# An order pass with measured durations, turns in a PSUM tile and a new table of key shifts

## The chip, the cores and the metric

The kernel runs on one core of a Trainium2 chip. A core has five engines with queues of their own: TensorE (PE in the profile; PEld is its weight load), VectorE (DVE), ScalarE (ACT), GpSimd (POOL) and SyncE (SP), which here issues the DMAs. The metric is the time of one execution on the device in microseconds (us).

## The reference

The computation has three parts in a row. The matrices are held in fp32, the weights of the expert layers in 64-bit floats.

```
# attention: q, k, v are 2 x 8 x 1152 x 64; pairs of query rows are averaged (576 rows remain)
q_pool = q.reshape(B, H, S // 2, 2, D).mean(axis=3)
attn   = softmax(q_pool @ k.T / sqrt(D));   x = attn @ v          -> 1152 tokens x 512
# first expert layer: w_in 512 x 2048, w_out 2048 x 512
h = x @ w_in
P = a0 + a1*h + a2*h^2 + a3*h^3;   Q = 1 + |b0|*|h| + |b1|*h^2
x = (P / (Q + 1e-6)) @ w_out
# second expert layer: w_gate and w_val 512 x 1536, w_out 1536 x 512
xn = x / sqrt(mean(x*x) + 1e-6) * rms_g
out = (silu(xn @ w_gate) * (xn @ w_val)) @ w_out
```

## The kernel before

All instructions are written through a scheduling pass in the kernel's own Python. Each piece of work is an `Op` with an engine, a cost in nanoseconds, a key, a function that emits the instructions, the operations it depends on, and the buffers it uses. Some operations have several ways, that is several engines with a cost each. The pass (`order`, from line 398) keeps a clock per engine: it works out when each ready operation could begin (`begin`: the ends of what it depends on plus a hand-over time between the two engines, and the time at which its buffers come free), and emits, engine by engine, the ready operation with the smallest key among those that could begin about as early as the first. What is emitted is a fixed order for every engine; on the chip each engine takes its queue in that order and waits on semaphores. So costs, hand-overs and keys change no instruction, but the order of each queue, and for operations with several ways the engine.

Two long strings steer the pass. `SHIFTS` has a sign per operation, in the order of their creation, which moves the operation's key by a multiple of 250; `WAYS` has a point where the pass may choose the way, or a digit that pins it. 226 of 2624 entries are digits.

`Buf.serial` marks a buffer whose users on different engines take turns in the pass: its last user's end and a hand-over delay the next (in `begin`). Before the change, the tiles `prep`, `av` and `accp` are so marked, and the PSUM tile `hid` of a hidden layer is not.

The stages, in order of time:

- Attention, in 72 tiles of 128 query rows by 1152 keys, two heads to a pair and nine tiles to a pair of heads. Per tile: scores on PE (line 851, into `hid`), the row maximum on DVE (`nm`, line 880), the exponential on ACT (`p`, line 886), transposes on PE (line 902), copies to SBUF (`pt`) on ACT (line 934) or DVE (line 937), and the product with V on PE (`av`, line 1006). PE's order of these is written out: `attention()` chains all of a pair's score, transpose and V operations by dependences. Not in that chain are the transposes of keys and queries (`prep`, line 800) and of the reciprocal sums. Two `hid` tiles alternate.
- Beside the attention the expert weights are loaded and split from 64-bit floats into a high and a low part (lines 175 to 236; `W_STEPS`, `S_STEPS`): those of the first layer beyond the first few are written back to DRAM ("spill") and fetched later.
- First expert layer (`rational`): 16 hidden units of 128 columns by 1152 tokens. PE makes the hidden tile (`hid`, three matmuls per product since high and low parts are multiplied); ACT and DVE read it in turn (lines 1195 and 1198 on ACT; 1201, 1204 and 1211 on DVE), then work on in SBUF (1214 to 1235), and ACT and POOL (or DVE) make the high and low part of the result (1243, 1246). PE multiplies these by `w_out` into `accp`, and DVE adds that to `acc` (line 1301). For the first two units (`FINE`) and two others the work goes by thirds of 384 columns, each in a PSUM bank of its own, declared independent by bank.
- Norm (`norm`, lines 1356 to 1405): squares, a sum on PE, a root on ACT and four small POOL operations (`o_nr`), broadcast by PE.
- Second expert layer (`gated`, `out2`): 12 units of the same size.

PE works on fp32r operands; a 384-column matmul of the expert layers takes about 0.17 us from start to start.

Of the kernel before, what the change touches and what calls it, by code (L numbers as in the profile page):

```python
# [19 lines left out]
def attention_moe_moe2_kernel(  # L20
# [18 lines left out]
    nc = tc.nc  # L39
    B, H, S, D = q.shape  # L40
# [8 lines left out]
    NU2 = DFF2 // 128  # L49
# [207 lines left out]
    S_STEPS += [("ACT", 625, s_hi), ("POOL", 1230, s_lo), ("SP", 1460, s_store)]  # L257
# [3 lines left out]
    if wide:  # L261
        W_STEPS += [("ACT", 680, w_abs), ("DVE", Port(345), w_shift), ("DVE", Port(620), w_sign), ("DVE", Port(620), w_rest)]
# [13 lines left out]
    def weight(w, u):  # L276
# [13 lines left out]
        "]ZAOQF(:O/TPHZGUPNQOPjLPR=?P@PKSPcPPXSPKEPPI]8PYLPZPPC]WB<POPTPDRPPYLUCFHLm=JPJLV`*JP1PPXMPP<PPWFKPP"  # L290
        "alKWPEcj[DO]PIHPNTFJPZFMHM/,aSPP8GVPWJLQ]KKLRHPYITdcPLhcCiPPZMPXXbP:<LL[>[_PT_PPRCPPPNaPH=MCPPRL;PZK"
        "P[T]QKRK@KOQ@CS_U@O/QXMQ_J9PQS`PIMPX^>6APdYFPLPvPMKCFVRON:ZE]CiLNCcPPyD>PO[XCLXfkPG^PP^WZSFP_E0T2kSN"
        "IMb(PPMMPPYPPPd4J:HP(PXPy8VQMTPSEMIE8RPQQbG>`UANARWOcNPP]LSPN]NNQJt;JwPMOPV]hCPUNUVQF__YPlPOthUPYS<]"
        "PH]YYP[U`(VT;QNNUsY]NA_FXZAPPWJSXTRVQCPbPPZWGFhTPVMbkhTJVP>eY>PJLPPPPOTY2PE]PPFSOVFDJNNQ>PCYPa;iPBPS"
        "[PfPL^TATPXP=LWP_B<OY>P=PVI6WaPXKPcPTPYPhZPOPPaSHPHPJPOPEERRfJX`2TdOaOVPHM^5TUOUPbPPdQPJK[>ORH6P@PBJ"
        "QQKOQDPYPHNZCSFRPOKEWPEPUGPPMPCaP_bPPPbQKFZEWaPKPCZUPRPPVEMV7R[`QRPPR_GOQHQ5PDeU`C?BLNW^O+T^PIPHNRSK"
        "PPMIPPPGPY`PfvLPPRRRPUJU:GLXV^MZLPY^IycPESiP=TJ^PPaTRQ/PZ>-EKIPmcPE;NKOEvuPJFnNQH`TCTUeUBMYPSH;?6OSZ"
        "PVSW[PP9W>_IOgUJ^mOQ3GNDTPKIPhFP[RPBVIJP[6^<XJwPPPSYEVBI.PWARQPQULDDJZJWTSf1NW=FPPKkeFWPJPQP8aPFPOBF"
        "PX@V>RIETfGPKPWPSLPI(^JqIIPaPYSPlNP^PAPn)]G`ZPRNEWPU<]y9PPRNyRAFPDA;EV^W^P?NIW]PMJ^UTPTIKKLUPbUS_MO["
        "NYc]WPRNIIPPPKIQUJPVFDTCKIPPuHM<TPHbT[VKF[QhMWPPPKPWLtYE_aPaNaoR_JVlMPPfrQPPPPWL>RPKUPKEPQLI(PV:H^RJ"  # L300
        ";SENX(GP7Pd9]F^TU[MP5MHQbP_PTV7PZ:XJP(=UNPP_PdPYP?[POHBTUFLOM[KNWVXK;SwNU;L2TP[C[PPj>XUJPPMPJ]@LF`ZM"
        "KWv]P_^QdGb.aWE[[JIPTKJVQ2ITEOAP0]PIRL_O7LZE@^QBLPPXON`:TMKgOQPRFPPNPjKbPTSNSEPP@P<uTPJXWOQPOb`VPe@P"
        "FUQfPUPXPPTPKUGF>jLCI^MEZ=JPSOP?IZVPeP(GMRPSMLnVJPPUPPK;PJKOB9`VGP(Q[LZPLKZEPRMTHWPPNPQCGPPHFY9LYPBP"
        "^GO@fPW[UQirIRULJPPPMPRSPSQPH^SZHPG=TQ(OXYOV=ADPWPWLhVTKYQKHRUP?XZ^cPNN5PQZR.DYP6]^XLQNVAWY;CUP`QPPL"
        "QNOKPNbEOPPPFaPWEIfPPZMPPUI=OPZCPQ<d;IPQWCPRMOQe`NH>PRQHPBPOQH`WNP@PVMP`JPfJTNPR_Pe<PJPJMPXPCVPPOP:P"
        "KOJPVcIOnhPyPQPPXKPILPUPZ=PfPMhMJP9bPPDJPSPJFPfQZ=ZTWPRKPKOHPRTNS@PQKPLUJQSPT3RYoPVVUPP>PIQDMPVnNXPD"
        "PPR`OOPVPBOT]^VAGFMLOiHPPJcLIMPQKRYPYFd`P?WUOPMPY?PQPKUXXS_Z[RdP@PNQUIm`ePPRX_XPxPLHPPXPAPLSPJO;ohYy"
        "POSO`P[E7PP2LMZ(PNaMPMyVRn]CLRRXJ=MGPFSJEP3pPPPE@PXZPPpPSQSaPhfYUPJPaLRX[PSEZIU>USIYUP(PA<KPJPfPIPPI"
        "OPWPxPPPL3GC^URLUQOIPMQLPIU8J5tXPbIWPP=qGUJTUCPPPDLV^VPUT_BVPNK@PPPIOPM9H[DP^PPOPMfPGXPN_J]?@APPKVQE"
# [398 lines left out]
    def head_ops(i):  # L708
# [30 lines left out]
        def f_add(eng):  # L739
# [6 lines left out]
            [(POOL, 1500, lambda: f_add(nc.gpsimd)), (DVE, Port(cost(DVE, m)), lambda: f_add(nc.vector))],  # L746
# [84 lines left out]
    def tile_ops(i):  # L831
# [62 lines left out]

        NB = NKT - 1
# [700 lines left out]
```

## Time and profile before

| | us |
|---|---|
| median of 3 runs (lowest to highest) | 708.67 (706.51 to 709.95) |
| the profiled execution | 706.74 |
| its span, first to last instruction | 705.0 |
| PE busy | 683.8 (97%) |
| PEld busy | 595.3 (84%) |
| DVE busy | 544.1 (77%) |
| ACT busy | 397.0 (56%) |
| POOL busy | 246.6 (35%) |

The shares are of the span. Busy time of PE is the time in which at least one matmul was in flight by its record; the records' ends are modelled, so a short wait may lie inside busy time. A wait is the idle time of an engine before an instruction, put down to whatever came last of what that instruction waited for. The attention takes the first 258 us, the first expert layer goes to about 434, the norm to 482, and the second expert layer to the end.

### The profile page before, as it was taken

The numbers are of one execution on the slowest core, as the hardware profiler recorded it, in microseconds if no ns is written. First come the engines' busy times: TensorE is split into PE (matmuls) and PEld (weight loads), VectorE is DVE, ScalarE is ACT, GpSimd is POOL, SyncE is SP. The second block draws the span as 40 slices with busy tenths as digits, with TensorE's granted clock in tenths as the row PEclk, the third lists the DMA queues.
The fourth block names the chain that finished last, engine by engine and source line by source line (L and its number), as shares of the span: only waits on it lengthen the run. The fifth ranks groups of instructions, "written<-read, shape, count | busy, mean of one in ns | idle before, by whom it ended". The sixth has DMA issues, their size and how long they took to land.

```text
span 705.0 us, 13072 instructions
## 1 busy us (share of the span) xinstructions
PE 683.8 (97%) x5257; PEld 595.3 (84%) x5257; DVE 544.1 (77%) x724; ACT 397.0 (56%) x624; POOL 246.6 (35%) x246
## 2 busy tenths in 40 slices
PE   8899999999999999999999999999999999999997
PEld 7576767667776778999999999999999899989996
DVE  5789998898888876999968989867778155983944
ACT  3676787888788876978646566346333232311310
POOL 1124346666546674311111253344222012422500
PEclk9999999999999999999999999999999999999999
DMA  7443436656555436115105005000325012340103
GB/s 209 127 130 101 142 100 193 197 177 228 176 189 181 157 125 215 60 61 164 44 24 186 31 6 174 31 1 1 119 91 160 20 60 89 91 150 0 60 1 134
DMA packets 53900, 77.66 MB, mean 110 GB/s; under 512 B 6480, under 2 KB 36176, under 8 KB 53840
## 3 DMA queue, kind: packets, MB, share of 16 engines
q1 hardware_dynamic: 53840, 76.83, 33.7%
q8 instruction: 41, 0.67, 0.4%
q14 instruction: 19, 0.16, 0.1%
HBM read 62.40 MB, written 14.42 MB: 109 GB/s over the span
## 4 chain that ended last, share of the span: by engine, by line
PE 76%; DVE 14%; ACT 7%; issue 2%; POOL 1%; DVEq 0%; ACTq 0%; POOLq 0%
PE hid L590 24%; PE accp L590 19%; PE hid L851 11%; PE av L1006 10%; PE hid L902 7%; PE prep L800 3%; DVE m_q L1211 2%; ACT p L886 2%; DVE m_p L1201 2%; DVE m_p L1204 2%; DVE m_q L1226 2%; DVE nm L880 1%; DVE m_p L1232 1%; ACT m_u L1195 1%; DVE m_p L1235 1%
## 5 line engine op out<-in xcount | busy, mean ns | idle before, releaser
L590 PE MATMUL hid<-x_hi,win_hi 128*128 128x384 f32 x480 | 161.2, 336 | 4.2 <-issue 2.1
L590 PE MATMUL hid<-x_hi,win_lo 128*128 128x384 f32 x480 | 160.6, 335 | 0.0
L590 PE MATMUL hid<-x_lo,win_hi 128*128 128x384 f32 x480 | 155.4, 335 | 0.0
L880 DVE TENSOR_REDUCE nm<-hid 128x1 f32<-128x1152 f32 x72 | 95.1, 1354 | 15.0 <-PE hid L851 14.6
L886 ACT ACTIVATE p<-hid,nm 128x1152 f32<-128x1152 f32 x72 | 87.9, 1221 | 29.5 <-DVE nm L880 29.3
L590 PEld LDWEIGHTS hid<-x_hi,win_hi 128*128 128x128 f32 x480 | 90.2, 188 | 6.6 <-issue 4.5
L851 PE MATMUL hid<-kT,qT 64*128 64x256 f32 (+3 forms) x800 | 94.0, 380 | 0.1
L590 PEld LDWEIGHTS hid<-x_lo,win_hi 128*128 128x128 f32 x480 | 89.6, 188 | 1.0
L590 PEld LDWEIGHTS hid<-x_hi,win_lo 128*128 128x128 f32 x480 | 90.1, 188 | 0.0
L902 PEld LDWEIGHTS hid<-ident,p 64*128 64x128 f32 x1296 | 52.7, 140 | 34.8 <-issue 13.7
L1246 POOL TENSOR_TENSOR g_lo<-m_p,g_hi 128x1152 fp32r<-128x1152 f32 (+1 forms) x16 | 37.8, 2368 | 125.8 <-ACT g_hi L1243 79.4
L851 PEld LDWEIGHTS hid<-kT,qT 64*128 64x128 f32 (+1 forms) x800 | 70.2, 182 | 9.1 <-issue 1.7
L1006 PE MATMUL av<-pt,vn 128*64 128x288 f32 x576 | 76.7, 411 | 0.0
L902 PE MATMUL hid<-ident,p 64*128 64x64 f32 x1296 | 66.2, 230 | 9.0 <-ACT p L886 8.3
L934 ACT ACTIVATE pt<-hid 128x512 f32<-128x512 f32 (+2 forms) x129 | 57.4, 473 | 24.7 <-PE hid L902 23.0
L175 ACT ACTIVATE wc<-wraw 128x512 f32<-128x512 f32 x68 | 45.8, 673 | 39.2 <-POOL win_lo L208 18.1
L590 PE MATMUL accp<-g_hi,wout_hi 128*128 128x384 f32 x192 | 65.3, 340 | 1.2 <-DVE acc L1301 1.2
L937 DVE COPY pt<-hid 128x512 f32<-128x512 f32 (+2 forms) x95 | 50.5, 548 | 18.7 <-PE hid L902 17.0
L590 PE MATMUL accp<-g_lo,wout_hi 128*128 128x384 f32 x192 | 64.3, 335 | 0.4 <-POOL g_lo L1246 0.4
L590 PE MATMUL accp<-g_hi,wout_lo 128*128 128x384 f32 x192 | 64.2, 335 | 0.0
L1006 PEld LDWEIGHTS av<-pt,vn 128*64 128x64 f32 x576 | 38.6, 136 | 27.0 <-issue 3.3
L1455 ACT ACTIVATE m_p<-hid 128x1152 f32<-128x1152 f32 (+1 forms) x14 | 14.0, 997 | 57.9 <-PE hid L590 57.8
(120 smaller groups left out, 1231.9 us busy)
## 6 DMA issues: line engine op xcount, KB each, us to landing
wraw<-in_moe_w_out_dram SPq DMA_DIRECT2D x28, 512.0 KB, 3.5
far<-spill SPq DMA_DIRECT2D x23, 512.0 KB, 3.1
wraw<-in_moe_w_in_dram SPq DMA_DIRECT2D x16, 512.0 KB, 3.9
wraw<-in_moe_w_gate_dram SPq DMA_DIRECT2D x12, 512.0 KB, 3.8
wraw<-in_moe_w_val_dram SPq DMA_DIRECT2D x12, 512.0 KB, 3.6
kn<-in_k_dram SPq DMA_DIRECT2D x16, 288.0 KB, 4.0
vn<-in_v_dram SPq DMA_DIRECT2D x16, 288.0 KB, 3.3
qn<-in_q_dram SPq DMA_DIRECT2D x16, 256.0 KB, 3.1
```

Of the source, the lines that this page charges most:

```text
L175: nc.scalar.activation(c.bitcast(F32), wt["raw", n][:, :, 1].bitcast(F32), AF.Abs, scale=2.0**-112)
L590: ins = nc.tensor.matmul(dst, lhsT=a[x], rhs=b[y], start=first and i == 0 and p == 0, stop=last and i == n - 1 and p == len(by) - 1,)
L800: seen(nc.tensor.transpose(ps[:, at:at + 128], src, ident))
L851: ins = nc.tensor.matmul(ps[to, j, c:c + x1 - x0], lhsT=qT[2 * pr + h][rows, c0:c0 + to.stop - to.start], rhs=kT[2 * pr + h][rows, x0:x1], ...
L880: nc.vector.tensor_reduce(out=e["nm"], in_=scores(), op=ALU.max, axis=AX.X, negate=True)
L886: nc.scalar.activation(e["p"], scores(), AF.Exp, bias=e["nm"], scale=1.0, accum_out=sums[pr][:, t:t + 1])
L902: ins = nc.tensor.transpose(ps[:, g, c:c + 64], e["p"][rows, 128 * j:128 * j + 128], ident[rows, rows])
L934: return nc.scalar.activation(to, src, AF.Copy)
L937: return nc.vector.tensor_copy(to, src)
L1006: nc.tensor.matmul(e["av", h][64 * c:64 * c + 64, 0:QW], lhsT=v_tile[2 * pr + h][:, KEYS[kt], :], rhs=pt[pr, h][:, kt, c * QW:(c + 1) * QW ...
L1201: by_bank(nc.vector.tensor_mul(as3(p_(), cs), as3(p_(), cs), h_()))
L1246: eng.tensor_sub(g_(1), p_(), g_(0).bitcast(F32))
```

## The change

The diff touches the pass and its inputs. No function that emits instructions is altered.

- Costs of operations: the weight steps, the query addition (`o_qa`), the row maximum, the exponential, the copies of the transposed tile on ACT and DVE, the spread of the reciprocals (`o_rx`), ACT's absolute value in the first expert layer (`o_aq`), POOL's low part (`o_lo`) and the norm's POOL chain (`o_nr`).
- Hand-over times become a table by pair of engines; a switch of PE between kinds of matmul is booked at 140 instead of 100.
- `project_ops` marks the hidden tile's buffer as serial unless the layer is one that goes by banks (`by_banks`).
- `SHIFTS` and `WAYS` are new throughout; 240 entries of `WAYS` are digits.

```diff
-            ("ACT", 680, w_abs), ("ACT", 680, w_pm), ("DVE", Port(345), w_shift), ("DVE", Port(620), w_rest_kept),
-            ("POOL", 1250, w_times),
+            ("ACT", 630, w_abs), ("ACT", 560, w_pm), ("DVE", Port(410), w_shift), ("DVE", Port(620), w_rest_kept),
+            ("POOL", 1310, w_times),
...
     SHIFTS = (
-        "]ZAOQF(:O/TPHZGUPNQOPjLPR=?P@PKSPcPPXSPKEPPI]8PYLPZPPC]WB<POPTPDRPPYLUCFHLm=JPJLV`*JP1PPXMPP<PPWFKPP"
+        "HPBOSTaTYHCTNONaP4PDPCZIPTuFM2oOLPPPZIUBDNPfPWPKUvXHI7Q<PNPLP@FLIR?UcUPPAPYPPfca]XUXPdAIjNNWPP[LPUPS"
...
-    SWITCH = 100
+    SWITCH = 140
...
+    HANDOFF = {
+        "PE": {"DVE": 220, "ACT": 200, "POOL": 150},
+        "DVE": {"PE": 250, "DVE": 110, "ACT": 92, "POOL": 221},
+        "ACT": {"PE": 265, "DVE": 118, "ACT": 110, "POOL": 190},
+        "POOL": {"PE": 110, "DVE": 55, "ACT": 120, "POOL": 65},
+        "SP": {"PE": 2110, "DVE": 2000, "ACT": 2000, "POOL": 2000},
+    }
+
     def handoff(a, b):
-
-        if a == b:
-            return {DVE: 127, ACT: 143, POOL: 96}.get(a, 0)
-        return 2000 if a == "SP" else {PE: 196, ACT: 160, DVE: 140, POOL: 75, "SP": 100}[a] + (110 if b == PE else 0)
+        return HANDOFF[a].get(b, 0 if a == b else 196 if a == "PE" else 100)
...
         ps = ps or Buf("hid")
+        ps.serial = not by_banks(w, u)
...
+    def by_banks(w, u):
+        return w == "in" and u in FINE or (w, u) in (("gate", 0), ("val", NU2 - 1))
+
     def bank_access(w, u, c, ins):
-        if w == "in" and u in FINE or (w, u) in (("gate", 0), ("val", NU2 - 1)):
+        if by_banks(w, u):
...
-            [(POOL, 1500, lambda: f_add(nc.gpsimd)), (DVE, Port(cost(DVE, m)), lambda: f_add(nc.vector))],
+            [(POOL, 1640, lambda: f_add(nc.gpsimd)), (DVE, Port(cost(DVE, m)), lambda: f_add(nc.vector))],
...
-        o_red = Op(DVE, 1350, key + -2500, f_red, o_qk, [nb])
-        o_exp = Op(ACT, 1430, key + 2400, f_exp, [o_red], [nb, pb, sb])
+        o_red = Op(DVE, 1300, key + -2500, f_red, o_qk, [nb])
+        o_exp = Op(ACT, 1263, key + 2400, f_exp, [o_red], [nb, pb, sb])
...
-                [(ACT, 70 + 1.09 * w + n2, lambda n_=n_: f_out(n_, by_act)), (DVE, 80 + 1.16 * w + n2, lambda n_=n_: f_out(n_, by_dve))],
+                [(ACT, 60 + 0.85 * w + n2, lambda n_=n_: f_out(n_, by_act)), (DVE, 80 + 1.03 * w + n2, lambda n_=n_: f_out(n_, by_dve))],
...
-        o_rx = Op(POOL, 1050, kr + 300, f_rx, [o_rinv], [rb, rxb])
+        o_rx = Op(POOL, 1200, kr + 300, f_rx, [o_rinv], [rb, rxb])
...
-            o_aq = Op(ACT, cost(ACT, n), k + 2000, f_aq, [o_q], [bq])
+            o_aq = Op(ACT, cost(ACT, n) + 110, k + 2000, f_aq, [o_q], [bq])
...
-            o_lo = Op(POOL, cost(POOL, n), k + 5000, f_lo, [o_hi], [bp, *g], [(DVE, Port(cost(DVE, n)), lambda: f_lo(nc.vector))])
+            o_lo = Op(POOL, cost(POOL, n) + 120, k + 5000, f_lo, [o_hi], [bp, *g], [(DVE, Port(cost(DVE, n)), lambda: f_lo(nc.vector))])
...
-        o_nr = Op(POOL, 400, key, f_nr, [o_ms, o_rs], [br])
+        o_nr = Op(POOL, 1050, key, f_nr, [o_ms, o_rs], [br])
```

## Rows read from the trace of the kernel before

**Rows 1.** Busy time (and instructions) of each engine by stage; PEclk is the granted clock.

```profile
0.00:32.00 32.00, 26.30 (x248) 21.47 (x248) 19.89 (x34) 15.02 (x29) 5.71 (x11) 0.89 0.57 161
32.00:258.00 226.00, 220.79 (x2603) 158.02 (x2602) 196.46 (x294) 179.12 (x342) 118.74 (x132) 1.00 0.51 165
258.00:300.00 42.00, 38.82 (x231) 35.83 (x232) 33.25 (x57) 32.47 (x56) 18.92 (x20) 1.00 0.37 126
300.00:434.00 134.00, 131.52 (x748) 128.97 (x747) 117.20 (x107) 87.17 (x81) 32.09 (x12) 1.00 0.26 86
434.00:482.00 48.00, 47.24 (x278) 45.81 (x276) 36.57 (x58) 21.46 (x36) 18.15 (x24) 1.00 0.08 25
482.00:700.00 218.00, 218.00 (x1153) 204.56 (x1154) 139.54 (x177) 61.74 (x83) 52.98 (x49) 1.00 0.24 75
700.00:705.00 5.00, 1.16 (x6) 0.62 (x4) 1.22 (x2) 0.00 (x0) 0.00 (x0) 1.00 0.42 157
```

**Rows 2.** Groups of instructions, 32 to 258 us: busy, mean ns, idle before and releasers.

```profile
L880 DVE TENSOR_REDUCE nm<-hid 128x1 f32<-128x1152 f32 x66 | 87.2, 1354 | 11.9 <-PE hid L851 11.5
L886 ACT ACTIVATE p<-hid,nm 128x1152 f32<-128x1152 f32 x66 | 80.6, 1221 | 24.2 <-DVE nm L880 24.0
L902 PE MATMUL hid<-ident,p 64*128 64x64 f32 x1187 | 59.8, 228 | 4.5 <-ACT p L886 3.7 <-DVE pt L937 0.2
L902 PEld LDWEIGHTS hid<-ident,p 64*128 64x128 f32 x1187 | 47.7, 139 | 28.0 <-issue 12.8 <-ACT p L886 7.4 <-DVE pt L937 3.7
```

**Rows 3.** Instructions in order of time near 87.7 us: start, length, idle before.

```profile
87.68 2.62 DVE L880 TENSOR_REDUCE nm<-hid 128x1 f32<-128x1152 f32 x2 [0.37 <-PE hid L851]
...
89.08 1.22 ACT L886 ACTIVATE p<-hid,nm 128x1152 f32<-128x1152 f32 x1 [1.54 <-DVE nm L880]
...
90.34 1.22 ACT L886 ACTIVATE p<-hid,nm 128x1152 f32<-128x1152 f32 x1
90.44 0.78 PE L902 MATMUL hid<-ident,p 64*128 64x64 f32 x17 [1.01 <-ACT p L886]
```

**Rows 4.** Waits of PE, 258 to 300 us: total, times, longest.

```profile
PE hid L590 <- issue: 1.2, 1, 1.2
PE hid L590 <- DVE m_p L1204: 1.2, 1, 1.2
PE hid L590 <- DVE pt L937: 0.9, 1, 0.9
```

**Rows 5.** Waits, 300 to 434 us.

```profile
DVE m_p L1204 <- ACT m_u L1195: 4.3, 4, 1.3
...
PE hid L590 <- issue: 0.9, 2, 0.5
```

**Rows 6.** Groups by form, 0 to 258 us: the 512-column copies.

```profile
L934 ACT ACTIVATE pt<-hid 128x512 f32<-128x512 f32 x81 | 46.9, 596 | 15.8 <-PE hid L902 15.0
L937 DVE COPY pt<-hid 128x512 f32<-128x512 f32 x62 | 42.2, 689 | 14.4 <-PE hid L902 13.2 <-ACT p L886 0.5
```

**Rows 7.** DVE in order of time at 287.8 us.

```profile
287.78 1.41 DVE L1211 SCALAR_TENSOR_TENSOR m_q<-m_u,absb,hid 128x1152 f32<-128x1152 f32 x1 [0.45 <-ACT m_p L1198]
```

**Rows 8.** Waits of PE, 434 to 482 us.

```profile
PE hid L1389 <- POOL small L1385: 0.6, 2, 0.4
```

**Rows 9.** Busy time in two stretches of the ramp (columns as in rows 1).

```profile
10.00:13.40 3.40, 1.57 (x33) 1.19 (x33) 2.75 (x4) 3.04 (x6) 1.54 (x1) 1.00 0.83 274
13.40:16.90 3.50, 3.50 (x29) 3.17 (x27) 1.38 (x3) 1.07 (x4) 0.00 (x0) 0.51 0.67 180
```

**Rows 10.** DVE and POOL in order of time at 397 us.

```profile
395.90 1.35 DVE L1201 TENSOR_TENSOR m_p<-m_p,hid 128x1152 f32<-128x1152 f32 x1
...
397.17 3.94 POOL L1246 TENSOR_TENSOR g_lo<-m_p,g_hi 128x1152 fp32r<-128x1152 f32 x1 [11.12 <-ACT g_hi L1243]
...
398.96 3.36 DVE L1226 SCALAR_TENSOR_TENSOR m_q<-m_q,m_u 128x1152 f32<-128x1152 f32 x1
```

**Rows 11.** Groups by form, 275 to 450 us.

```profile
L1226 DVE SCALAR_TENSOR_TENSOR m_q<-m_q,m_u 128x1152 f32<-128x1152 f32 x14 | 20.9, 1493 | 0.0
```

More of the change, by code (lines that the diff above doesn't have):

```diff
@@ L253, in attention_moe_moe2_kernel @@
         S_STEPS += [
-            ("ACT", 680, w_abs), ("ACT", 680, w_pm), ("DVE", Port(345), w_shift), ("DVE", Port(620), w_rest_kept),
-            ("POOL", 1250, w_times),
+            ("ACT", 630, w_abs), ("ACT", 560, w_pm), ("DVE", Port(410), w_shift), ("DVE", Port(620), w_rest_kept),
+            ("POOL", 1310, w_times),
         ]
-    S_STEPS += [("ACT", 625, s_hi), ("POOL", 1230, s_lo), ("SP", 1460, s_store)]
+    S_STEPS += [("ACT", 625, s_hi), ("POOL", 1170, s_lo), ("SP", 1460, s_store)]
     W_STEPS = [("SP", 1460, w_load)]
     if wide:
-        W_STEPS += [("ACT", 680, w_abs), ("DVE", Port(345), w_shift), ("DVE", Port(620), w_sign), ("DVE", Port(620), w_rest)]
+        W_STEPS += [("ACT", 560, w_abs), ("DVE", Port(410), w_shift), ("DVE", Port(620), w_sign), ("DVE", Port(620), w_rest)]
     W_STEPS += [("ACT", 620, w_hi), ("POOL", 1230, w_lo)]
@@ L295, in attention_moe_moe2_kernel @@
[L295 to L309, printed above, removed]
@@ new lines, in attention_moe_moe2_kernel @@
+        "OPZNpLDTSsCPROPPPQFIUPWYPPTXPkPx`B=KHpICXPPieO0PLWXMPBJLTGUTPK8RQQVfY+G4QQcQTRQ>P19UGQPPQLP]E^POP2<X"
+        ")RTPJahLL)TTOPSPOPT_POPQLMSeJ>WIBUHKXP]`PG@PKP8n(V3ZAdPGQMPPPP=QTVPVPYPVAaVTAYYPQS>KOB?PMOPaeI_cPG=I"
+        "?OWLPJPLPbPIXKIKGRPWREN]POPdPNXPNP]PXJ]JN`RWPPMSSP[DO[gfPN4_PSQTHPPRPAPPXPPNNPYYPU^HPSPnM[TRP[;bPPdU"
+        "G<YIPUZMMPNJPP8Pi3qYY*;HPPNTPPPwcPFPPJPOJf(M(SOOPO^PYTfNSbMeLfPDlbPPSYBgQ;JMPO8e`:WKPHPPRLTNPQPQUPTH"
+        "NES9JP=MHPIQPBIWEFPAWGQFTXPMPNNM1cPsPPRGCJVMPAMLPySD>Ke4(_P6PkLoNPYsFRPPDMQr`I[TTr^faRVOPDPECJRVPPN0"
@@ new lines, in attention_moe_moe2_kernel @@
+        "PVPTIPD1IYPDKYJR5P@b7_oDXdMYyCDIBWTFp>RNDCwZPO_VNMBOPVPEPPPH^WROScM`PBUHOSImJeYqK4QPMPlNggLKf^F^SWWR"
+        "ENVGcGXJWWL[^XNSPU`VPGPTPCNRPDQRPKNZIiSPCHS]PPdQUIPKZ8SP;SMRYbnYWfLKPd5[VSPUNW;PYE`SXDMId(OXOPPPIOGP"
+        "MVMYPMPiGHMULZ[M=XnOUWJUIOmP^A4UJKSJPPGSV9PGIPUL:PPKPmPQPPPPPRVVYPAQPdd;HMPPHsP<PCKPPPyEHP?FSPNrWR=R"
+        "PPOPTO>P_RPLUPMUP7GRViPDRnPM@DZ_jUC:cYIQPPIT`PPR<OTMNA=7_JDQPe`kNPO>IhXMGPQPIJ@erPWHPP=`PO^bMFPCVXXP"
+        "PGMNPpGKr@PQPRBHPE(L^PJPP9UOPPKKNVPJPPUYZKPP`PWlNPJLUFPV^OqJJ<LBbKAPFDMTLPJ@PPWPRdPSNPPZPL5XPHPUIPQH"
@@ new lines, in attention_moe_moe2_kernel @@
+        "L]`TPP:NPQPHNPXPIPTM=QPLEENPP.PXKYaAtyBPU[S;PVENZTPsPPfLLLZPOHC`l=PLPPKPUDPPAVVSPO?NLPWeSdPPLEQTyKP>"
+        "UQ@JPPPRVPOgKFiLcNPNM_PQPWVOZHFfNPPNORPSbPPKPPhKP^Y[GPO@JOKV0PVTPPPPFUPPOJMKc9@NsM7ePKPmHJ[PeU:OcPXS"
+        "^LC^P[APPPPpYJIJ]TPGWCISHBPRT]P8_cN7XPPLD[URkPUSHPPRPrDW;SOIVUPAWcP:QP6fJD:RLPPPSPKV?PPbnYSRRJ0FMNPP"
+        "OGCJPUBLZUfPXbGL^PSKGQXJPIpPZUTDP@RYLPAdQLabNaLPP[8NPJ@RP7HfPPXKPMPPOPL3APCPEPP+AvVXJ]EQLRPYPXOPVL^J"
+        "HcLPXTXPPMfIPGP.TMPiH^PNPWUJu=PPJNJHP[S`VKhYPPTR<P_ZDP[PBWH_kLHNMPI]Bl9QPBZIHLBPPPMFPPPPoI?NXH7[VPyY"
@@ new lines, in attention_moe_moe2_kernel @@
+        "VREPNPO^VjHGPPFWc`URTaPK(6PIAWRSPE]TYN^ahNSOPN4>KPI[NPFRQfLvXPPPNPGS`PbM6PSOPCaPWGNUQWPPWUYKYH(PLRNP"
+        "PPePRoPPKRSPPPPKPQLH@La3TB;TNARCRbPPPOULY^LKQSbQR^QOSKS`MW@@LiPLPPPSYNRPUWmQKLZPP8MUUH8ZiRLUVRSPT6>h"
+        "p(aWP>PLKZ@TJSLHP3SJPP[`NPQDKSGJPZPMDNPGPOfPGKd[?PRPPXP)@]BNS=JPP@PU^PPLPZIJSP]S`bBhPPIQLPPQKQPVSFPP"
+        "j<PPPVLPUZP]VPR^XOMBaXgSRRvWPZZPDIYbRPIEJPqPR@PET>;iPPOhUQMNPEPTPPTMfFMPPODHALAR<>`JQFL[PPPP(SVPPNQO"
+        "PQ^PCPhCSSYXRSJGQtPdPPUSYZUPUOYP`FQU<cVPcFPSPPBW^LHP[EGWJROOAa?NU]TPMP;LUTPbXAHSPPbPX5Z@=PFXXOT3gZ`C"
@@ new lines, in attention_moe_moe2_kernel @@
+        "0....................1.....1.0......0.10.....1.00.....1..0.......................0.................."
+        "...0........1..0.....0...................1........0......1.01.....1..............01.........0.....01"
+        "0.................1.....0..........0......1.0........0........1......1.0.....................0......"
+        "....00....01......1........1........1..0.......01.................0.......00........1.......00......"
+        ".....1..........0...............1........................0.10.....0.11.................0............"
@@ new lines, in attention_moe_moe2_kernel @@
+        "..0..............00.......................0.1.........1..............0..0........0........1........1"
+        ".......01.....0.1.......................0......0......0.1.........0.....0..0.....1.0........1......0"
+        "..0........1.......00.......1.............1.........0.......1.....0..........0......0........1......"
+        "..0.1......1.0.................1........1.......................11....010........0......11.....20..."
+        "..10.....1......0.......1......0.................................................1........1........."
```

49 lines of the change are left out of this document (17 added, 32 removed).

## The prediction

> **What bounds the kernel now.** Read first the table of busy time by stage [rows 1]. TensorE (PE) is busy 683.83 of 705.00 us. That table also says where it is not, and this is all that another order can win, since no instruction of PE is added or taken away. Before 32 us it is idle 32.00 - 26.30 = 5.70 us; in the rest of the attention 226.00 - 220.79 = 5.21; at the hand-over to the first expert layer 42.00 - 38.82 = 3.18; in the first expert layer 134.00 - 131.52 = 2.48; around the norm 0.76; in the second expert layer (482 to 700 us) 0.00; and in the tail 3.84. Sum 21.17 us, 3% of the span. In the same rows the reader sees who comes next: in the attention DVE with 196.46 of 226 us (87%) and ACT with 179.12 (79%), in the first expert layer DVE with 117.20 of 134 (87%), in the second nobody.
>
> Then the waits. In the attention after the ramp PE's largest wait is that of the transposes for the exponential, 3.7 us; the exponential in turn waited 24.0 us for the row maximum, and the maximum 11.5 us for the scores [rows 2]. The chain scores, maximum, exponential, transpose can be seen once in full at 87.7 us: two maxima in 2.62 us, begun 0.37 us after DVE had run dry, two exponentials 1.26 us apart, and PE 1.01 us idle [rows 3]. At the hand-over PE waits three times about a microsecond before a hidden tile, twice for a reader on DVE and once for nothing that the profile names [rows 4]. In the first expert layer its waits are short, 0.5 us the longest of those for a hidden tile [rows 5].
>
> **The change part by part.** No edit alters an instruction: they alter what the scheduling pass believes and prefers. Instructions move on their engines' queues, the DMA issues on SP's among them, and, where an operation has several ways, between DVE, ACT and POOL. PE's order of scores, transposes and attention-times-V is a chain of dependences that the diff leaves alone, so in the attention only the small transposes of keys, queries and reciprocals can move to fill PE's holes.
>
> *Durations.* The diff books the exponential at 1263 instead of 1430, the maximum at 1300 instead of 1350, the ACT copy of 512 columns at 60 + 0.85 x 512 = 495 instead of 628, DVE's at 607 instead of 674. The rows give the exponential's step from start to start as 90.34 - 89.08 = 1.26 us and the maximum's as 2.62 / 2 = 1.31 [rows 3]. Two maxima of 1354 ns by record [rows 2] thus take 2.62 us and not 2.71: records overlap by about 90 ns, and the copies of 596 and 689 ns [rows 6] occupy about 0.51 and 0.60. The new numbers are close to the trace. The old pass thus booked ACT too high in the attention by 72 x 0.167 + 81 x 0.133 = 22.8 us, and DVE by 72 x 0.05 + 62 x 0.067 = 7.8 us. It saw ACT full where ACT is at 79%, and left DVE, the engine that really is nearly full, with 62 of the large copies. The new one can move copies to ACT and sees true lengths of the chain. What PE can get from it is bounded by its 5.21 us. But DVE was already idle when the maximum of rows 3 became ready (0.37 us), so at such a place only a filler on PE helps, and the old pass with its longer exponential had reason to place one there. I take 2.0 of the 5.21; the ends are 0 and 5.2.
>
> *Turns in a PSUM tile.* At 287.78 us DVE's m_q waits 0.45 us for ACT's m_p (line 1198), whose result it does not use: both read the hidden tile, and one goes after the other [rows 7]. In the first expert layer DVE's line 1204 waited 4.3 us in 4 waits for ACT's line 1195, again another reader of that tile [rows 5]. The old pass did not know of this; the new one plans around it. It cannot free more PE time than PE loses: 3.18 at the hand-over, where 1.2 and 0.9 us of it hang on DVE's reading of the tile [rows 4], and 2.48 after. The two first layers are read by thirds, which the diff leaves without turns, so at the hand-over the gain must come from a better order of DVE's 33.25 busy us. I take half of each: 1.6 and 1.2; the ends are 0 and 3.2, 0 and 2.5.
>
> *Norm and remaining constants.* The norm's POOL chain is booked at 1050 instead of 400; PE's wait for it is 0.6 us [rows 8], of 0.76 idle. I take 0.3. The switch of PE's mode (140 for 100), the cost of the query addition, of the spread reciprocals and of the weight preparation belong to engines with room: POOL is busy 118.74 of 226 us in the attention, and in the second expert layer PE loses nothing. I cost them at 0, with rival 3 below for where their cover ends.
>
> *The ramp.* Before 32 us there is nothing else to do while the first chains run. After a stretch in which PE was busy only 1.57 of 3.40 us, 3.5 us went by at a granted clock of 0.51, that is at 1.2 instead of 2.4 GHz [rows 9]; the 0.89 of the whole ramp [rows 1] is two of these, 2 x 3.5 x 0.49 = 3.4 of 32 us. A new order can win or add one such stretch, 3.5 x 0.49 = 1.7 us either way. I take 0.
>
> *The table made anew.* It holds as many entries as before; 240 instead of 226 pin a way. How good the search was can't be read from anything here; this is why I take about half of what is open and not all.
>
> Sum: 2.0 + 1.6 + 1.2 + 0.3 = 5.1 us, nothing in the second expert layer and in the tail (the last eviction and store remain). The profiled execution took 706.74 us; it becomes 701.6. The median of the runs shown is 708.67, on which the same sum gives 703.6. Not knowing which of the two the next median resembles, I predict the middle, 702.6. Half a per cent, 3.5 us, is about what a measurement here can tell from no change: the three runs alone spread over 3.4 us. The bounds of the parts give from 0 to 5.2 + 3.2 + 2.5 + 0.8 + 1.7 = 13.4 us of gain, and 1.7 of loss.
>
> **The rivals.**
>
> 1. *More is open than PE's idle time shows.* PE's ends are modelled, so short holes hide in busy time. The weight loads show them: in the attention they waited 7.4 us for the exponential and 3.7 for a DVE copy, 11.1 against PE's 3.9 for the same two [rows 2]. If half of the 11.1 and all of 3.18 + 2.48 + 0.76 come back, the gain is 12.0 us, and the time on the middle scale 695.7. Beside this the Trainium skill, "Perfetto Trace Analysis", section "Identifying the Most-Contended Engine", says that TensorE's headroom is to be judged by the busy share of its weight loads and not by that of its matmuls. By that rule the attention with 158.02 of 226 us (70%) has far more room than the second expert layer with 204.56 of 218 (94%). I follow it only so far: an attention load of 0.14 us stands for a matmul of other shape than an expert one, so the share differs without any hole. Against the rival: the chain at 87.7 us shows PE waiting on latency, not on order.
>
> 2. *Nothing to be seen.* What the pass gets right lies beside PE's path: the turns delay DVE by some microseconds, but DVE has 134 - 117.20 = 16.8 us free in that stage, and PE's waits are many short ones that another order only puts elsewhere. For it: PE at 97%. Time: 708.
>
> 3. *Slower: DVE and POOL block each other in the first expert layer.* At 397 us POOL's g_lo and DVE's m_q (line 1226) overlap; m_q takes 3.36 us where a 1152-column step that meets nobody, that at 395.90, took 1.35, so one meeting costs DVE 2.0 us [rows 10]. The group's mean of 1493 ns over 14 shows that such meetings are rare in this order: 14 x (1.493 - 1.35) = 2.0 us in all, one such meeting [rows 11]. The new pass redraws which operations meet, and books POOL longer by 120 without moving it. DVE stands before PE here through the hidden tile's release and the accumulator's additions; the layers' buffers take up one delay, so it decides from about the fourth further meeting in neighbouring layers on. With six meetings more, 12 us on DVE, of which half are taken up, the kernel is 6 us slower: 714. The Trainium skill, "SBUF — State Buffer", section "Who interferes with whom", says that DVE with two SBUF inputs and POOL hold their shared port for a whole instruction and that the order of issue decides who is blocked. By that rule a new order alone can bring this rival; the trace agrees, since m_q has two SBUF inputs. Against it: the pass carries such a term, before and after.
>
> **How the numbers follow.** Forecast (698 to 705) 0.49; rival 1 (below 698) 0.10; rival 2 (705 to 712, by the noise also a small gain or loss) 0.26; rival 3 (above 712) 0.15. Faster by over half a per cent means below 705.1: 0.49 + 0.10 = 0.59, of which I give 0.01 to the border; same 0.27; slower 0.15. For 8 in 10 the range runs from 695.5, which takes in rival 1's own time, to 712, which leaves out rival 3.
>
> **What the profile after would show.** If right: PE idle at 32 to 258 us down to about 3.2, at the hand-over to about 1.6, no wait of PE for a hidden tile over a microsecond there; more than 81 large copies on ACT and fewer than 62 on DVE; DVE's wait of 4.3 us on line 1204 mostly gone; the second expert layer and the tail unchanged. Rival 1 shows as weight loads in the attention waiting less than 7.4 us for the exponential. Rival 3 shows as means of lines 1226 and 1232 well above 1.5 us together with PE waits for DVE. The forecast is wrong if PE's idle time outside ramp and tail (11.6 us) does not fall by three or more, or if the time moves by more than this idle time does.

## The result and the profile after

The kernel after takes 699.29 us (median of 6 runs, 696.55 to 700.77), the kernel before beside it 709.62 (6 runs, 706.51 to 711.56): a ratio of 0.985, 95% interval 0.982 to 0.988. It is faster, and the predicted 702.6 is 3.3 us too high. The time lies inside the predicted range, but that range (695.5 to 712) is wide and held the kernel before as well. On another chip a replay of the same queues took 699.8 against 705.64, a ratio of 0.992 (0.990 to 0.994). The medians of before differ by the clocks that its executions were granted and by a meeting of two engines, told of below. At about one clock (0.995 in the mean over the span for before, 0.994 for after) the second chip's runs of before lie at 706.8 to 707.3 and those of after at 699.1 to 700.0. The profiled executions agree: 706.74 against 699.88, 6.9 us less.

Where the time went is read from three moments in the timeline of PE (start, length, operation, idle before): the first hidden matmul of the first expert layer, and the first and last matmul that projects its result into `accp`. First before, then after.

```profile
258.76 0.41 PE L590 MATMUL hid<-x_hi,win_hi 128*128 128x384 f32 x1 [0.89 <-DVE pt L937]
...
284.55 0.33 PE L590 MATMUL accp<-g_hi,wout_hi 128*128 128x384 f32 x1
...
473.85 0.33 PE L590 MATMUL accp<-g_hi,wout_lo 128*128 128x384 f32 x1
```

```profile
257.57 0.44 PE L596 MATMUL hid<-x_hi,win_hi 128*128 128x384 f32 x1 [0.45 <-ACT pt L943]
...
283.52 0.33 PE L596 MATMUL accp<-g_hi,wout_hi 128*128 128x384 f32 x1
...
467.21 0.34 PE L596 MATMUL accp<-g_hi,wout_lo 128*128 128x384 f32 x1
```

The attention ends 1.2 us earlier. From the first hidden matmul to the first projection it is 25.8 us before and 25.9 after: nothing. From the first projection to the last it is 189.3 and 183.7: 5.6 us, most of the 6.9. Behind it the stages keep their lengths (231.2 and 230.9 us to the end). In the table of busy time by stage, the counterpart of [rows 1], the stages are cut where after has them:

```profile
0.00:32.00 32.00, 25.69 (x243) 21.01 (x245) 19.89 (x36) 14.52 (x28) 2.64 (x9) 0.89 0.60 173
32.00:257.00 225.00, 219.63 (x2609) 158.03 (x2605) 200.13 (x290) 189.42 (x369) 116.51 (x123) 1.00 0.52 167
257.00:300.00 43.00, 40.81 (x245) 37.56 (x242) 33.03 (x55) 31.70 (x56) 10.64 (x12) 1.00 0.36 118
300.00:430.00 130.00, 130.00 (x752) 129.87 (x751) 116.22 (x105) 88.25 (x83) 28.86 (x12) 1.00 0.26 86
430.00:475.00 45.00, 44.38 (x262) 43.36 (x261) 37.08 (x58) 20.73 (x34) 16.19 (x21) 1.00 0.08 24
475.00:693.00 218.00, 218.00 (x1156) 204.59 (x1155) 137.65 (x186) 63.06 (x87) 40.87 (x38) 1.00 0.24 75
693.00:698.10 5.10, 1.28 (x6) 0.74 (x4) 1.34 (x2) 0.00 (x0) 0.00 (x0) 0.86 0.41 154
```

The second number in a row is PE's busy time, the third that of the weight loads. In the first expert layer PE is idle for 0.00 us, where it was for 2.48. That is less than half of the 5.6 us. The rest is in the third number: the loads were idle for 134.00 - 128.97 = 5.03 us before [rows 1], and are for 0.13 after. Most short holes lay under the modelled ends of matmuls, and the loads, which run back to back here, showed them. Between the first and the last projection the loads are busy for 181.84 us before and for 182.26 after, and idle for 7.46 and 1.43: the stretch is as long as the loads' work, which stays, and their holes, which go. In the attention PE is idle for 5.37 us, and was for 5.21. ACT works 10 us more there and DVE 4 us more; PE's idle time hardly moves with it.

The waits of the first expert layer from 300 us on (engine and line, what it waited for, total, times, longest) say who sets the pace. PE has none left; those of [rows 5] were the counterpart. Lines after are 9 higher.

```profile
ACT m_u L1204 <- PE hid L596: 16.6, 6, 8.3
...
ACT m_q L1223 <- DVE m_q L1220: 6.2, 5, 2.6
DVE acc L1310 <- PE accp L596: 5.2, 5, 2.5
DVE m_q L1220 <- ACT m_u L1204: 3.7, 2, 2.8
```

The wait of 4.3 us of DVE's third reading for ACT's absolute value (L1204 for L1195 before) is gone. A smaller one, 3.7 us, stands at the second polynomial's reading (L1220), which needs the absolute value itself. ACT and DVE now wait for PE. At the hand-over (257 to 300 us) the three waits of [rows 4] have become 1.3, 0.4 and 0.4:

```profile
PE hid L596 <- DVE m_p L1213: 1.3, 1, 1.3
PE hid L596 <- ACT pt L943: 0.4, 1, 0.4
PE hid L596 <- issue: 0.4, 1, 0.4
```

In the attention the waits and groups of [rows 2, 6] have these counterparts (32 to 257 us; the copies from 0 to 257): PE still waits for the exponential, 4.0 us, and of the large copies ACT makes 83 for 81 and DVE 59 for 62. Over the whole program, with the small ones, eight went from DVE to ACT (129 to 137 on ACT, 95 to 87 on DVE).

```profile
L911 PE MATMUL hid<-ident,p 64*128 64x64 f32 x1187 | 60.0, 228 | 5.3 <-ACT p L895 4.0 <-DVE pt L946 1.0
```

```profile
L943 ACT ACTIVATE pt<-hid 128x512 f32<-128x512 f32 x83 | 47.6, 596 | 7.1 <-PE hid L911 6.3
L946 DVE COPY pt<-hid 128x512 f32<-128x512 f32 x59 | 39.7, 688 | 13.6 <-PE hid L911 7.2 <-ACT wraw L215 3.6 <-ACT wc L175 1.6
```

### The profile page after: what moved, and what is told of

It is laid out like the page before. It is cut to its first block, busy times and chain, and to the rows that moved or that the text cites. A ratio compares the mean times of both kernels' runs of the same rounds, so it can differ in the third digit from the quotient of the medians.

```text
span 698.1 us, 13067 instructions
## 1 busy us (share of the span) xinstructions
PE 679.8 (97%) x5257; PEld 595.2 (85%) x5257; DVE 545.3 (78%) x728; ACT 407.7 (58%) x652; POOL 215.7 (31%) x214
## 4 chain that ended last, share of the span: by engine, by line
PE 88%; DVE 5%; ACT 4%; issue 1%; DMA 1%; SPq 0%; POOL 0%; DVEq 0%; ACTq 0%; POOLq 0%
PE hid L596 35%; PE accp L596 24%; PE hid L860 10%; PE av L1015 9%; PE hid L911 7%; PE prep L809 3%; ACT p L895 2%; DVE nm L889 2%; DVE pt L946 1%; DMA qn<-in_q_dram 1%; PE prep L1062 0%; ACT pt L943 0%; DVE qp L751 0%; DVE acc L1404 0%; DVE m_p L1210 0%
## 5 line engine op out<-in xcount | busy, mean ns | idle before, releaser
L1255 POOL TENSOR_TENSOR g_lo<-m_p,g_hi 128x1152 fp32r<-128x1152 f32 (+1 forms) x15 | 34.0, 2272 | 124.2 <-ACT g_hi L1252 96.2
L943 ACT ACTIVATE pt<-hid 128x512 f32<-128x512 f32 (+2 forms) x137 | 60.4, 470 | 16.0 <-PE hid L911 14.6
L946 DVE COPY pt<-hid 128x512 f32<-128x512 f32 (+2 forms) x87 | 46.3, 556 | 16.0 <-PE hid L911 9.2
L208 POOL TENSOR_TENSOR win_lo<-wc,win_hi 128x512 fp32r<-128x512 f32 x17 | 23.2, 1367 | 96.8 <-ACT win_hi L201 87.0
```

The lines of the kernel that those rows point to most:

```text
L208: eng.tensor_sub(lo, w_float(n), hi.bitcast(F32))
L943: return nc.scalar.activation(to, src, AF.Copy)
L946: return nc.vector.tensor_copy(to, src)
L1255: eng.tensor_sub(g_(1), p_(), g_(0).bitcast(F32))
```

## The experiments

In most of these kernels the pass does not choose: it replays a list of operations, each with the way that was taken, recorded from the pass of before or of after. So a part of one order can be put into the other, or one operation exchanged with its neighbour. The replay of after unchanged is the last pair below. Line numbers of such kernels are higher; operations and tiles are the same. "Before" stands for the runs of the kernel before on the same chip: 708.77 us (25 runs) for e1_att, e2_rest, t_before and t_after; 708.53 (19) for flat_old, flat_new, c_before and fill_after; 705.64 (18, the second chip) for dve_light, att_light, again_after and fill_again. A ratio compares all runs of a set and is not always that of the two medians.

**The two halves apart.** e1_att takes the attention's queues from after and the rest from before, e2_rest the other way round.

```diff
-            (each step picks the best ready operation by begin() and key)
+            e1_att:  QUEUES = after's entries of the attention, then before's of all the rest
+            e2_rest: QUEUES = before's entries of the attention, then after's of all the rest
```

> Every engine's queue up to the end of the attention as in the changed kernel, every queue after it as in the kernel before (the two orders are written out and replayed, nothing else differs). Theory (the gain lies in the first expert layer): the first hidden matmul of the expert layers starts about 1.2 us earlier as in the changed kernel, and all of the rest keeps the holes of before; 1.2 us faster than before. Rival (an earlier or otherwise ordered attention sets up the expert layer): 4 us or more faster.

> The reverse: queues of the attention as before, queues after it as in the changed kernel. Theory (expert layer): PE without a hole from 300 to 434 us, 5.6 us faster than before, the end of the attention unchanged near 258.8 us. Rival (the two halves only work together): under 3 us faster, with PE holes in the expert layer.

e1_att: 705.94 us (12 runs), ratio 0.998 (0.996 to 1.000), 0.0021 x 708.77 = 1.5 us below before. The interval reaches no change at all, and the 1.2 us of one pair of profiles can't carry it either: one and the same queue of before's attention brought the first hidden matmul at 256.86 to 259.01 us in five profiles (before, t_before, c_before, e2_rest, dve_light), with a clock in the first 32 us of 0.89 to 1.00. Runs at one clock show it better. At 0.995 those of before fall into two groups, 706.4 to 706.9 and 708.6 to 709.0 us, and those of e1_att into 705.7 to 705.8 and 707.4 to 707.8: 0.9 and 1.2 us less. So the attention's share is about 1 us. In its profile the first expert layer still has holes, and one is large. DVE and POOL in order of time, and the matmul that was late:

```profile
395.48 2.66 POOL L1352 TENSOR_TENSOR g_lo<-m_p,g_hi 128x1152 fp32r<-128x1152 f32 x1 [11.11 <-ACT g_hi L1349]
395.48 3.87 DVE L1338 SCALAR_TENSOR_TENSOR m_p<-m_p,ncoef,m_u 128x1152 f32<-128x1152 f32 x1
...
399.28 0.54 DVE L1407 TENSOR_TENSOR acc<-acc,accp 128x384 f32<-128x384 f32 x1
...
399.87 0.44 PE L693 MATMUL accp<-g_hi,wout_hi 128*128 128x384 f32 x1 [2.29 <-DVE acc L1407]
```

This is the meeting of [rows 10], in which the same two operations began within 10 ns of each other. [rows 10] has POOL's, at 397.17 us; DVE's, in the kernel before, is this one:

```profile
397.16 1.41 DVE L1232 SCALAR_TENSOR_TENSOR m_p<-m_p,ncoef,m_u 128x1152 f32<-128x1152 f32 x1
```

There DVE's step came through in 1.41 us and POOL's took 3.94. Here POOL took 2.66 and DVE 3.87: the addition behind DVE's step came late, and PE stood for 2.29 us. Before has this coin toss in its order; its profiled execution had won it.

e2_rest: 706.19 us (12 runs, one of them of 2030 us for no reason that is known), ratio 0.997 (0.995 to 0.999), 2.3 us below before. The total missed the 5.6 us that were expected, the layer did not. From 300 to 434 us its row, and the waits at its seam (257 to 300 us):

```profile
300.00:434.00 134.00, 134.00 (x775) 133.88 (x774) 120.22 (x109) 91.03 (x86) 28.92 (x12) 1.00 0.25 87
```

```profile
PE hid L693 <- DVE m_p L1310: 6.4, 1, 6.4
DVE m_p L1307 <- ACT m_p L1304: 5.1, 1, 5.1
...
ACT wc L175 <- DMA wraw<-in_moe_w_gate_dram: 3.6, 1, 3.6
```

The layer runs without a hole, 183.7 us from first to last projection as in after, so its 5.6 us come from its own order and not from the attention's. But where the two recorded halves meet, a weight step on ACT now stands ahead of the layer's first steps and waits 3.6 us for its DMA. PE stops for 6.4 us, until 281.65, and from 277.0 to 284.5 us, over the stop and behind it, the granted clock was 0.54. The seam ate more than half of what the layer won.

**The turns alone.** t_before takes before and moves ACT's absolute value forward in 5 units, so that it comes first; t_after takes after and delays it in 6 units.

```diff
 five units of t_before, by operation (p: polynomial steps 1 to 3; abs: ACT's |x|)
-    p1, p2, abs, p3
+    abs, p1, p2, p3
 six units of t_after
-    abs ahead of p2
+    p2, abs, p3
```

> Kernel before with one kind of move: in five hidden units of the first expert layer, in which ACT's abs of the hidden tile stood between DVE's second and third reading of it, abs is put ahead of all other readings; only five places of ACT's queue differ. Theory (turns in the PSUM tile delayed DVE, and through it PE): DVE's wait of 4.3 us on its line of the third reading falls under 1 us, PE's holes in the layer shrink, 2 to 5 us faster than before. Rival (holes come from PE's own order or from the accumulator's additions): DVE's wait falls, the time stays within 1 us of before.

> Changed kernel with the opposite move: in six hidden units abs is put between DVE's second and third reading of the tile. Theory (turns): DVE waits some 4 to 6 us more for ACT at its readings of the tile, PE gets holes in the first expert layer, 2 to 5 us slower than the changed kernel. Rival (the order as a whole, with slack on DVE, made the gain): within 1 us of the changed kernel.

t_before: 705.07 us (8 runs), ratio 0.994 (0.992 to 0.996). The time fell, but not for the reason under test. The layer's first to last projection takes 189.2 us, as before, and its loads stay idle for 134.00 - 129.21 = 4.79 us. The wait that was aimed at did go, from 4.3 to 0.2 us. It came back one reading earlier, where DVE was idle for 3.6 us before and is for 7.5 (group of the second reading, 300 to 434 us):

```profile
L1298 DVE TENSOR_TENSOR m_p<-m_p,hid 128x1152 f32<-128x1152 f32 x11 | 14.9, 1350 | 7.5 <-ACT m_p L1295 6.1 <-ACT m_u L1292 1.4
```

What it gained is the lost tosses: in its profile POOL's step begins at 396.15 us, 0.97 us behind DVE's at 395.18, which takes 1.41 us, so nothing is left to chance there. At a clock of 0.998 its runs (704.6 to 705.2) lie beside the one of before (704.73), and at 0.997 (705.0 to 705.3) 2.4 us under before's (707.5 to 707.6). That the layer gets faster when this wait for a turn is taken away fell in this form.

t_after: 714.46 us (6 runs), ratio 1.007 (1.005 to 1.010) to before, some 15 us slower than after; far more than the 2 to 5 that were expected. Its layer takes 198.5 us from first to last projection. Its waits from 300 to 440 us:

```profile
ACT m_u L1301 <- DVE m_p L1307: 13.7, 4, 7.5
...
DVE m_q L1317 <- ACT m_u L1301: 10.1, 5, 3.6
...
PE hid L693 <- issue: 4.7, 2, 4.4
...
PE accp L693 <- DVE acc L1407: 2.4, 3, 0.8
PE accp L693 <- POOL g_lo L1352: 2.3, 1, 2.3
```

ACT's absolute value waits 13.7 us for its turn behind DVE's second reading (L1307), DVE's reading for the second polynomial (L1317), which needs that value, waits 10.1 us for it, and this reaches PE. The order of turns decides a lot; the one move of t_before does not find a better one.

**The table.** Both passes without it: every shift and way neutral.

```diff
-    SHIFTS = ( ... )      WAYS = ( ... )
+    SHIFTS = "P" * 2624   WAYS = "." * 2624
```

> Kernel before with its table taken out: no shift of any key, no way pinned; the old durations and hand-overs alone make the order. Both theories: 2 to 4 per cent slower than before (723 to 737 us). It is the reference for the next one.

> Changed kernel with its table taken out in the same way: new durations, hand-overs and turns alone. Theory (the pass judges better, whatever the table): 5 us or more faster than the old pass without a table. Rival (the gain is the table's, found under the new durations): within 3 us of the old pass without a table.

flat_old (durations and hand-overs of before): 715.09 us (5 runs), ratio 1.010 (1.007 to 1.014). flat_new (those of after, and the turns): 714.65 (6 runs), ratio 1.009 (1.005 to 1.012). By these numbers the two can't be told apart, but the runs differ in clock: at 0.995 two of flat_new (712.3 and 712.4) lie 2.8 us under the one of flat_old (715.2), so a few microseconds of gain from the new beliefs are not excluded. The layer hardly has it: in the profiles it takes 190.7 us from first to last projection for flat_old and 189.9 for flat_new, against 183.7 with the new table. The table found under the new beliefs makes most of the gain: it is worth some 15 us to the new pass, where the old table was worth 6.6 to the old one. Whether the search would have found it under the old beliefs was not tried.

**The meeting at 397 us.** c_before takes before and exchanges one addition with the step behind which it was late.

```diff
 one place on DVE's queue
-    t step, addition to acc
+    addition to acc, t step
```

> Kernel before with one exchange on DVE's queue in the first expert layer, at 397 us: the addition to the accumulator goes ahead of the 1152-column step that meets POOL's low part there. Theory (in most executions of before POOL wins that meeting, the step takes 3.9 instead of 1.4 us and the addition behind it keeps PE waiting 2.3 us; in the profiled one DVE won): about 2 us faster in the median than before, and no execution with the hole. Rival (the executions of before differ only by the granted clock near the start): within 0.7 us of before.

c_before: 705.25 us (12 runs), ratio 0.997 (0.995 to 1.000). The meeting is still there, lost by DVE, and now it is nobody's concern:

```profile
395.24 0.54 DVE L1398 TENSOR_TENSOR acc<-acc,accp 128x384 f32<-128x384 f32 x1
395.24 2.67 POOL L1343 TENSOR_TENSOR g_lo<-m_p,g_hi 128x1152 fp32r<-128x1152 f32 x1 [11.12 <-ACT g_hi L1340]
...
395.70 3.42 DVE L1329 SCALAR_TENSOR_TENSOR m_p<-m_p,ncoef,m_u 128x1152 f32<-128x1152 f32 x1
```

At a clock of 0.995 before's runs beside it fall into two groups, 706.3 to 706.9 and 708.5 to 709.2, 2.2 us apart, as long as PE's 2.29 us; c_before's lie at 705.9 to 706.6. At 0.997 it is the same: 704.9 and 705.3, 707.4 and 707.5 for before, 705.1 to 705.4 for c_before. The profiled runs agree: before's, which had won the meeting, took 706.74 us, in the lower group, and e1_att's, which had lost it, 707.38, in the higher group of its own. On the second chip before's runs at 0.995 are all at 706.8 to 707.3, but at 0.999 three are at 703.7 to 703.9 and two at 705.9 and 706.2.

**DVE's load.** dve_light takes before and leaves out one DVE step per unit in SBUF (`f_m`), so that part of the polynomial's quotient is not computed.

```diff
             def f_m():
-                stt(q_(), q_(), 1.0 + 1e-6, u_(), op0=ALU.add, op1=ALU.mult)
+                return
```

> Kernel before, all queues as they are, with one of DVE's SBUF steps (1.35 us) per hidden unit of the first expert layer left out (the result is not the reference's). Theory (PE's holes in the first expert layer come from DVE being behind, whatever held it): no holes of PE from 300 to 434 us, the layer 4 to 6 us shorter, first to last accumulation matmul 184 instead of 189 us. Rival (PE's own order or POOL's low part makes the holes): the layer within 1.5 us of before.

dve_light: 703.53 us (10 runs), ratio 0.997 (0.995 to 0.998).

```profile
300.00:434.00 134.00, 133.19 (x765) 132.00 (x764) 104.11 (x99) 89.20 (x83) 30.04 (x13) 1.00 0.27 90
```

With DVE at 104.11 us instead of 117.20, the loads' idle time in this window falls from 5.03 to 2.00. Over the whole way from first to last projection less is won: 187.3 us for 189.3, where 184 was expected, and 5.17 us of idle loads for 7.46. So a lighter DVE closes about a third of the holes, and part of that may be the meeting at 397 us, since the step left out is the one of 3.36 us in [rows 10]. After closes nearly all of them (1.43 left) with DVE at 116.22 of 130 us (89%), so the order counts for more than DVE's load.

**The attention's load.** att_light takes after and leaves out the conversion of those weights of the first layer that are spilled.

```diff
-            w_abs, w_pm, w_shift, w_rest_kept, w_times    for the spilled weights
+            the raw words, passed on
```

> Changed kernel's queues; the conversion of the weights that are written back during the attention is left out (their high words are split as they are, so two ACT, two DVE and one POOL instruction per weight are gone; the results of the expert layers are not the reference's). Theory (the attention's remaining holes are the latency of maximum, exponential and transpose on PE's fixed order, which no load explains): attention ends within 3 us of 257.6 us, PE's waits for the exponential between 32 and 257 us stay near 4 us. Rival (load on DVE and ACT bounds the attention): it ends 8 us or more earlier.

att_light: 699.39 us (3 runs) beside 699.80 for the replay of after, ratio to before 0.992 (0.989 to 0.994). The row of its attention, and PE's waits there:

```profile
32.00:257.00 225.00, 219.58 (x2608) 157.79 (x2604) 176.17 (x247) 163.55 (x325) 87.87 (x102) 1.00 0.53 168
```

```profile
PE hid L1017 <- ACT p L1001: 3.8, 5, 1.1
PE hid L1017 <- DVE pt L1052: 1.0, 2, 0.8
```

24 us less on DVE, 26 on ACT, and PE's idle time (5.42 us) and its five waits for the exponential (4.0 us in after, 3.8 here) stay. The first hidden matmul comes at 257.12 us, at 257.16 in the replay of after. So the weights' share of DVE's and ACT's load does not make these holes. The reading that is left, the latency of the chain scores, maximum, exponential, transposes on a written-out order of PE [rows 3], was not tested by itself.

**The ramp's clock.** fill_after and fill_again are after with 6, 6 and 3 idle matmuls of 128 columns into a PSUM tile that nobody reads, ahead of the transposes of the tiles 0, 2 and 4, where PE waits; again_after is the replay of after alone.

```diff
+            if i in FILL:
+                ps_ = T("av", [128, 512], F32, space=PSUM)
+                for _ in range(FILL[i]):
+                    nc.tensor.matmul(ps_[:, 0:128], lhsT=ones, rhs=ones, start=True, stop=True)
...
+    FILL = {0: 6, 2: 6, 4: 3}
```

> Changed kernel with 6, 6 and 3 idle matmuls into an unused PSUM bank ahead of the transposes of tiles 0, 2 and 4, where PE waits 1.8, 1.9 and 1.0 us for the exponential in the ramp. Theory (those holes are what lets the clock fall to 1.2 GHz in two stretches of 3.4 us): clock 1.00 in the ramp, 2 to 3 us faster than the changed kernel. Rival (the ramp is bound by the chain of maximum and exponential, so a slower PE costs nothing there): within 0.7 us of it, or slower if the added matmuls outlast the waits.

> The changed kernel again (its order written out and replayed), on the same chip as the next, to compare them: 699 us in the median, spread over some 4 us with the granted clock, the shortest at a clock of 0.999.

> The changed kernel with the idle matmuls in the ramp again. Theory (they keep the clock at 2.4 GHz): clock 0.999 or more in every execution, 697.5 us in the median, spread under 2 us; 1.5 to 2 us below the changed kernel on the same chip. Rival (the first comparison was chance between chips): within 0.5 us of it.

fill_after: 697.58 us (6 runs, 696.28 to 697.89), ratio 0.985 (0.982 to 0.988). On one chip, again_after 699.80 (699.14 to 700.42), ratio 0.992 (0.990 to 0.994), and fill_again 697.67 (5 runs, 696.18 to 697.97), ratio 0.989 (0.987 to 0.990): 2.1 us less than after without overlap of the runs, and the best version. Two stretches of the ramp, first again_after, then fill_again:

```profile
10.00:13.40 3.40, 1.82 (x27) 1.27 (x25) 3.10 (x5) 2.64 (x5) 0.00 (x0) 1.00 0.92 302
13.40:16.90 3.50, 3.50 (x33) 3.14 (x35) 2.03 (x5) 1.57 (x4) 2.02 (x1) 0.58 0.16 51
```

```profile
10.00:13.40 3.40, 2.66 (x36) 2.17 (x36) 3.11 (x5) 2.76 (x5) 0.20 (x1) 1.00 0.98 309
13.40:16.90 3.50, 2.73 (x35) 2.12 (x37) 3.50 (x5) 1.46 (x4) 1.34 (x1) 1.00 0.40 123
```

PE busy for 1.82 of 3.40 us was followed by a granted clock of 0.58, near the lower of the two levels (1.2 GHz); busy for 2.66 us, by 1.00. The one run of after that had a mean clock of 0.999 without fillers took 696.55 us, inside the range of the runs with them, so the clock is enough to explain the fillers' gain; one run can't rule out a small cost of the fillers themselves.

## Why the prediction was right, and where it was wrong

- **Faster, by an order in which DVE is less late: right** in sign. The wait of DVE's third reading went, the second expert layer and the tail stood still, and the copies moved towards ACT (83 and 59 for 81 and 62). That the turns as such bring it is not shown: moving them alone (t_before) left the layer at 189.2 us, and the new pass without its table at 189.9.
- **By one of its own signs the forecast was wrong.** PE's idle time outside ramp and tail had to fall by three or more, and fell from 11.6 to 8.2; but the time was not to move by more than that, and it moved by 6.9 in the profiled pair, twice as much. So the time landed in the range while the premise failed that PE's idle time is all that an order can win.
- **First expert layer, 1.2 us with 2.5 as its end: mis-sized; it gave 5.6.** The failing step is "It cannot free more PE time than PE loses". PE's idle time was taken as the loss, although the weight loads' 5.03 us idle stood in the same row [rows 1]. The loads measure it: 7.46 us of their idle time between the projections became 1.43, and the stretch 5.6 us shorter. Rival 1 had the idea but looked for it in the attention, where its own sign failed: the loads there wait 9.6 us for the exponential, not less than 7.4. The Trainium skill, "Perfetto Trace Analysis", section "Identifying the Most-Contended Engine", tells to judge headroom by the loads' busy share. In this stage the trace agrees (5.03 us idle, 5.6 won); in the attention, at 70%, it did not pay: their 68 us idle are 67 now, and in the second expert layer, at 94%, the 13.4 us stayed.
- **Attention, 2.0 us: about 1 came,** by e1_att's runs at one clock. It did not come as PE idle time up to the end of the attention, which was forecast to fall to 3.2 and is 5.37. 0.44 us of it is the wait right ahead of the first hidden matmul, 0.89 before and 0.45 after, which the prediction had counted in the hand-over. What shortened the rest is not settled: the stage's matmul records can hide as much.
- **Hand-over, 1.6 us: nothing came** but those 0.44. PE's idle time fell from 3.18 to 2.19, not to 1.6, one wait of 1.3 us for a reader on DVE was left, and the way from the first hidden matmul to the first projection did not shorten.
- **Norm 0.3: 0.76 idle became 0.62, 0.1. Ramp 0: right,** a clock of 0.89 in both; the two half-clock stretches that were priced at 3.4 us gave 2.1 when filled.
- **Rival 3 was real, and already there.** It put the meeting of DVE and POOL on the side of the new order. In fact before's own order had a meeting that costs 2.2 us when DVE loses it, and the one profiled execution had won it: the m_q of 3.36 us that the prediction read met POOL's step as the second, the first was the step at 397.16. After has meetings too, one of 3.29 us, but DVE is ahead of what PE needs and PE does not wait:

```profile
343.97 2.68 POOL L1255 TENSOR_TENSOR g_lo<-m_p,g_hi 128x1152 fp32r<-128x1152 f32 x1 [21.08 <-ACT g_hi L1252]
...
344.58 3.29 DVE L1235 SCALAR_TENSOR_TENSOR m_q<-m_q,m_u 128x1152 f32<-128x1152 f32 x1
```

- **The sum** of 5.1 stood against 6.9 in the profiled pair: one term at a fifth of its size, the others too high. That the total came near is in part luck. What the first set of runs shows above that (10.3) has two parts that one profile can't show: before's lost tosses of 2.2 us, and lower clocks (in the later sets before's runs of 709.4 to 711.6 us are nearly all those granted 0.993 or less).
- "How good the search was can't be read from anything here" was the honest place of doubt: flat_old and flat_new put most of the gain there.

## What to carry to other kernels

Where loads run back to back, size the gain of a better order by the idle time of the weight loads and not by that of the matmuls; where the stage mixes matmul shapes and waits on a latency chain, the loads' idle time promised here what neither the new order nor a lighter load gave. Look for two engines that begin within nanoseconds of each other on a shared resource with a due addition queued behind: here such a toss made runs of one kernel differ by its whole price, and one exchange on a queue took the price away. Taking away the wait that a profile names can just move it to another reading, as in t_before, unless the engine as a whole gets ahead. And compare profiles and runs of like clock: one queue's attention ended up to 2.2 us apart between executions.

## What the runs showed of the hardware

- Of DVE's and POOL's 1152-column steps that began within 10 ns of each other, the same pair took 1.41 and 3.94 us in one run and 3.87 and 2.66 in another. The Trainium skill, "SBUF — State Buffer", section "Who interferes with whom", has the order of issue decide; the trace agrees, and adds that at such a distance one order of the queues can come out either way.
- Fifteen small idle matmuls raised the granted clock of the first 32 us from 0.89 to 1.00, and the runs then lie within 1.8 us.
- The same instructions with two engines' turns in a PSUM tile exchanged cost some 15 us (t_after).
